# Scores of both key halves as one run of twelve products in a top-k attention and maxout kernel

## The chip, the cores and the metric

The kernel runs on one core of a Trainium2 chip. Its engines are TensorE (PE in the rows, with its weight loads as PEld), VectorE (DVE), ScalarE (ACT), GpSimd (POOL) and SyncE (SP, which issues the transfers). The metric is the device time of one execution in microseconds.

## The reference

Attention keeps the 32 largest scores of each row and drops the others; a three-way maxout layer and an output layer follow.

```python
def _attn_ref(q, k, v):                      # 8 batches, 8 heads, 576 rows, head size 64
    B, H, S, D = q.shape
    top_k = 32
    scale = 1.0 / np.sqrt(D)
    scores = scale * np.matmul(q, k.transpose(0, 1, 3, 2))
    kth = np.partition(scores, -top_k, axis=-1)[..., -top_k:-top_k + 1]
    mask = scores >= kth
    scores = np.where(mask, scores, -1000000000.0)
    scores = scores - np.max(scores, axis=-1, keepdims=True)
    attn = np.exp(scores)
    attn = attn / (np.sum(attn, axis=-1, keepdims=True) + 1e-09)
    return np.matmul(attn, v).astype(np.float32)

def _moe_ref(x, w1, w2, w3, w_out):          # x 4608 x 512, w1 to w3 512 x 768, w_out 768 x 512
    h = np.maximum(np.maximum(x @ w1, x @ w2), x @ w3)
    return (h @ w_out).astype(np.float32)
```

## The kernel before

The attention is cut into 160 units, 20 in each batch: four pairs of heads times five query tiles. The first four tiles of a pair hold 128 queries of each of its two heads (a full unit); the fifth holds the last 64 queries of both heads in one tile of 128 rows (a narrow unit). Unit 70, of which rows of the order are shown below, is the first tile of the third head pair of the fourth batch.

A unit goes through these steps, with the letter that the planner's table gives each and the line that does the work:

- **q, scores (L511).** The 576 keys are taken in two halves of 288. One half is six matmuls: for each of two heads the products high·high, high·low and low·high of split queries and keys. A half fills one score tile in PSUM, 128 x 2 x 512 floats, of which 288 columns of each head are used. There are two such tiles (the ring `s`), so that two halves are in flight at most.
- **e, copies (L522; L525 to L529 for a narrow unit)** by ACT, from the score tile to SBUF, one for each half. **s, sweeps (L539)** by DVE: the eight largest of every 72 keys, eight MAX8 for each half of a full unit, read from the score tile itself. A narrow unit's sweeps read the copies. A score tile is free again when its copy and, in a full unit, its sweep are done.
- **N, p1 to p5 (L545 to L570):** a pivot for each row out of the sweeps, on POOL and DVE. **g (L577, ACT), w (L582, POOL), k (L586, DVE):** signs of the scores against the pivot, the scores below it, their eight largest. **i, j, h (L594 to L606):** the 32nd largest is picked.
- **m, mask (L629, DVE)** and **x, exponential (L638, ACT)**; **d, r, z** (L645, L650, L657): the denominator.
- **T, transposes (L696, L691, L693, PE)**, **E, their copies (L711 to L716, ACT)**, **v, values (L741, PE)** for two full tiles together, **y, Y, Z** (L751 DVE, L756 ACT, L764 POOL): the row of x that the next layer reads, in two halves of fp16.

Before each pair of heads PE transposes its queries and keys (L454, L463). The maxout layer (L797) and the output layer (L857) of a batch are PE work with short steps on the other engines (L804 to L812, L862); they start when the x of their batch is there. The weights are decoded, measured and cut in two within the first units (L241 to L305).

The program's order is written out by a planner, `in_order`, when the kernel is built. Each step is a `Piece` with its engine, a cost in ns, the pieces that it needs, the rings that it takes a buffer of, and a rank (the unit's number plus an entry of `OFFSETS`). The planner keeps a clock for each engine, takes the piece that can start first, and lets a piece of lower rank go ahead of one that could start up to `PATIENCE` ns earlier. A piece that takes a buffer can start when that buffer's last readers are done by the planner's clock. The two layers' pieces are a list of their own, `fill`, from which PE takes when no piece of the attention can start soon enough. PE's pieces have a mode: `rows` for the scores (64 rows of the array for each of two heads), `columns` for the values, none for the rest; a change of mode costs `SWITCH` ns in the plan. DVE pieces marked `alone` (p4 on L568, the masks on L629) are planned to start no earlier than POOL's end plus `LOCK_A`, which is negative. Each engine then runs its own list in that order, and waits by semaphores.

In `attention`, which writes the pieces of one unit, each half of the scores is a piece of 393 ns that takes one buffer:

```python
        for i in range(2):
            rel = []
            takes = [("s", rel)]
...
            p(("q", i), "PE", 393, lambda i=i: qk(n, i), needs=needs, takes=takes, mode="rows")
```

Of the kernel before, what the change touches and what calls it, by code (L numbers as in the profile page):

```python
# [30 lines left out]
SWITCH = 95.0  # L31
WINDOW = 150
LEAD = 8.0
LOCK_A = -150.0
LOCK_B = -100.0
OFFSETS = {'x1': 0.96, 'j': 0.85, 'i': 0.48, 'N': 0.29, 'w1': -0.04, 'e1': -1.05, 'y': 0.91, 's1': 0.01, 'v': -0.12, 'u': -0.09, 'p1': -0.14, 'g0': 0.06, 'h': -0.01, 'E2': 0.48}
RANK_P = -3.5
RANK_R = 4.0
AHEAD = 4
RANK_W = (-2.0, 0.0, 1.0, 4.0)  # L40
RANK_V = -12.0
# [85 lines left out]
        left -= 1  # L127


PATIENCE = {'PE': 119.0, 'DVE': 50.0, 'ACT': 0, 'POOL': 50.0, 'SP': 0.0}  # L130


@with_exitstack
def kernel(ctx, tc, q, k, v, moe_w1, moe_w2, moe_w3, moe_w_out, out):
# [350 lines left out]
    books = {}  # L485
# [13 lines left out]
    def qk(n, i):  # L499


        b, hp, u = units[n]
        qT, kT = T_of[b, hp]
        if i == 0:
            open_unit(n)
        s = ps_s.tile([P, 2, 512], F32, name="s")
        for n_, (qa, ka) in enumerate(((0, 0), (0, 1), (1, 0))):
            for h in range(2):
                sl = slice(64 * h, 64 * h + 64)
                c0 = u * P if u < NU else S - 64 * (1 + h)  # L510
                nc.tensor.matmul(s[:, h, :HALF], qT[sl, qa, c0:c0 + P], kT[sl, ka, i * HALF:(i + 1) * HALF], start=(n_ == 0),  # L511
                                 stop=(n_ == 2))
        st[n]["s"].append(s)
# [385 lines left out]
    n = len(units)  # L899
# [5 lines left out]
    preps, starts, prep_of = [], [], []  # L905
# [5 lines left out]
    def attention(n):  # L911

        b, hp, u = units[n]
        nt = 2 if u < NU else 1
        full = nt == 2
        g = group_of.get(n, [n])
        opens, closes = n == g[0], n == g[-1]
        d = of[n] = {}
        p = lambda key, *a, **kw: d.setdefault(key, piece(*a, rank=n + OFFSETS.get(key if isinstance(key, str) else key[0] + str(key[1]), 0.0), **kw))
        for i in range(2):  # L920
            rel = []
            takes = [("s", rel)]
            needs = list(prepared[prep_of[n]])
            if i == 0 and b not in opened:
                opened[b] = []
                takes.append(("books", opened[b]))
            if i:
                needs.append(d["q", 0])
            p(("q", i), "PE", 393, lambda i=i: qk(n, i), needs=needs, takes=takes, mode="rows")
            p(("e", i), "ACT", 519 if full else 700, lambda i=i: evac(n, i), needs=[d["q", i]] + ([d["e", 0]] if i else []),  # L930
              takes=[] if i else [("ssb", held(n, "ssb"))])
            p(("s", i), "DVE", 1112 if full else 536, lambda i=i: sweep(n, i),
              needs=([d["q", i]] if full else [d["e", 1] if x else d["e", 0] for x in range(2)] if i else [])
              + ([d["s", 0]] if i else []), takes=[] if i else [("L", held(n, "L"))])
            rel.append(d["e", i])
            if full:
                rel.append(d["s", i])
# [21 lines left out]
        for t in range(nt):  # L959
            p(("m", t), "DVE", 820, lambda t=t: mask(n, t), needs=[d["h"]], alone=True)  # L960
            p(("x", t), "ACT", 760, lambda t=t: expo(n, t), needs=[d["m", t], d["p2"]] + ([d["x", 0]] if t else []),
              takes=[] if t else [("pm", held(n, "pm")), ("rs", held(n, "rs")), ("sums", held(n, "sums"))])
# [11 lines left out]
        for i in range(3):  # L974
            if i == 1 and not full:
                continue
            rel = []
            p(("T", i), "PE", 436 if i < 2 else 218, lambda i=i: turn(n, i),
              needs=[xs[i]] + last_v if i < 2 else [*xs, d["z"], *([] if full else [d["u"]]), *last_v], takes=[("tr", rel)])
            first = opens and i == 0  # L980
            p(("E", i), "ACT", 466 if i < 2 else 264 if full else 453, lambda i=i: turned(n, i),
              needs=[d["T", i]] + ([] if i == 0 else [d["E", 0]]), takes=[("pT", held(g[0], "pT"))] if first else [])
# [6 lines left out]
        rel, takes = [], []  # L989
        needs = [x for k in g for key, x in of[k].items() if key[0] == "E"] + [scaled_v[b], loaded_v[b, hp]]  # L990
# [18 lines left out]
    def held(n, *key):  # L1009
        return holders.setdefault((n, *key), [])  # L1010
# [104 lines left out]
    with tc.If(redo != 0):  # L1115
        with tc.For_i(0, B, 1) as b:
# [6 lines left out]
            for hp in range(NP):  # L1123
# [5 lines left out]
                for u in range(NU + 1):  # L1129
                    i = len(units)  # L1130
# [52 lines left out]
```

## Time and profile before

| | us |
|---|---|
| median of 2 runs | 1374.88 (1374.14 to 1375.62) |
| the profiled execution | 1373.02 |
| its span, first to last instruction | 1371.2 |
| PE busy | 1212.2 (88%) |
| DVE busy | 1200.0 (88%) |
| ACT busy | 1115.9 (81%) |
| POOL busy | 989.1 (72%) |

The span is what the views below divide. 1.8 us of the execution's time lie outside it. The busy time of an engine is a sum over its instructions, and stretches of the program differ: the first 150 us hold the weights, the last 70 us only the two layers of the last batch.

### The profile page before, as it was taken

The numbers are of one execution on the slowest core, as the hardware profiler recorded it, in microseconds if no ns is written. First come the engines' busy times: TensorE is split into PE (matmuls) and PEld (weight loads), VectorE is DVE, ScalarE is ACT, GpSimd is POOL, SyncE is SP. The second block draws the span as 40 slices with busy tenths as digits, with TensorE's granted clock in tenths as the row PEclk, the third lists the DMA queues.
The fourth block names the chain that finished last, engine by engine and source line by source line (L and its number), as shares of the span: only waits on it lengthen the run. The fifth ranks groups of instructions, "written<-read, shape, count | busy, mean of one in ns | idle before, by whom it ended". The sixth has DMA issues, their size and how long they took to land.

```text
span 1371.2 us, 32398 instructions
## 1 busy us (share of the span) xinstructions
PE 1212.2 (88%) x9981; PEld 859.8 (63%) x9981; DVE 1200.0 (88%) x5928; ACT 1115.9 (81%) x2732; POOL 989.1 (72%) x1669
## 2 busy tenths in 40 slices
PE   2331699899689999999999999999999999999997
PEld 1221477566467675676777676767676767776775
DVE  6797798999989999999999999999999999999621
ACT  3556799888898898898988899989988999898721
POOL 2779887678777787786787777778778768686511
PEclk9965899999789999999999999999999999999999
DMA  6341010211101011111111110201020101100000
GB/s 214 114 144 34 3 36 19 60 28 27 43 2 44 27 43 34 27 27 44 27 43 28 43 24 22 60 24 46 9 53 25 36 19 41 27 9 1 17 17 27
DMA packets 107893, 53.69 MB, mean 39 GB/s; under 512 B 91840, under 2 KB 100032, under 8 KB 107712
## 3 DMA queue, kind: packets, MB, share of 16 engines
q1 hardware_dynamic: 107712, 51.54, 13.9%
q8 instruction: 81, 1.33, 0.4%
q14 instruction: 100, 0.82, 0.2%
HBM read 42.07 MB, written 9.44 MB: 38 GB/s over the span
## 4 chain that ended last, share of the span: by engine, by line
PE 60%; DVE 19%; ACT 13%; POOL 3%; issue 3%; SPq 1%; DMA 0%; ACTq 0%; DVEq 0%; POOLq 0%
PE m L797 24%; PE tr L741 9%; PE s L511 9%; PE m L857 8%; PE tr L696 7%; DVE L L539 6%; DVE ssb L629 3%; ACT pm L638 3%; ACT w L577 3%; DVE Q L586 2%; ACT pT L711 2%; ACT ssb L522 2%; PE tr L463 2%; DVE ob L242 1%; PE tr L691 1%
## 5 line engine op out<-in xcount | busy, mean ns | idle before, releaser
L582 POOL TENSOR_TENSOR w<-ssb,w 128x576 f32<-128x576 f32 x288 | 416.3, 1450 | 57.3 <-ACT w L577 53.2
L797 PE MATMUL m<-xh,wall 128*128 128x256 f16 (+2 forms) x2448 | 438.3, 279 | 0.7 <-ACT ob L862 0.4
L797 PEld LDWEIGHTS <-wall 128*128 128x128 f16 x3672 | 339.4, 98 | 84.2 <-issue 14.5
L797 PE MATMUL m<-xl,wall 128*128 128x256 f16 (+2 forms) x1224 | 335.3, 279 | 0.3 <-POOL xl L764 0.3
L539 DVE MAX8 L<-s 128x8 f32<-128x72 f32 x2048 | 307.3, 223 | 19.9 <-ACT ssb L522 9.9
L629 DVE SCALAR_TENSOR_TENSOR ssb<-ssb,kth 128x576 f32<-128x576 f32 x288 | 257.1, 908 | 1.0
L638 ACT ACTIVATE pm<-ssb,nb 128x576 f32<-128x576 f32 x288 | 223.9, 778 | 27.0 <-DVE ssb L629 24.1
L511 PE MATMUL s<-kT,qT 64*128 64x288 f32 x1920 | 210.8, 334 | 32.6 <-ACT ssb L522 16.5
L586 DVE MAX8 Q<-w 128x8 f32<-128x576 f32 x288 | 214.9, 749 | 18.1 <-POOL w L582 18.0
L577 ACT ACTIVATE w<-ssb,Q 128x576 f32<-128x576 f32 x288 | 222.7, 777 | 9.5 <-DVE Q L570 4.9
L711 ACT COPY pT<-tr 128x512 f32<-128x512 f32 (+1 forms) x416 | 210.1, 521 | 20.8 <-PE tr L696 15.1
L696 PE MATMUL tr<-ident,pm 128*128 128x128 f32 x1152 | 182.0, 287 | 26.4 <-ACT pm L638 19.2
L511 PEld LDWEIGHTS s<-kT,qT 64*128 64x128 f32 x1920 | 144.3, 194 | 96.9 <-ACT ssb L522 28.5
L522 ACT COPY ssb<-s 128x576 f32<-128x576 f32 x256 | 161.5, 642 | 33.3 <-DVE L L539 17.0
L741 PE MATMUL tr<-pT,vt 128*64 128x256 f32 (+1 forms) x1920 | 183.2, 338 | 3.3 <-ACT pT L716 2.0
L696 PEld LDWEIGHTS tr<-ident,pm 128*128 128x128 f32 x1152 | 133.4, 145 | 73.3 <-ACT pm L638 32.6
L806 DVE SCALAR_TENSOR_TENSOR h<-m,rises,h 128x256 f32<-128x256 f32 (+2 forms) x204 | 100.6, 493 | 66.5 <-PE m L797 61.9
L741 PEld LDWEIGHTS tr<-pT,vt 128*64 128x64 f32 x1920 | 110.2, 139 | 66.0 <-issue 18.9
L812 POOL TENSOR_TENSOR hl<-h,hh 128x256 f16<-128x256 f32 (+2 forms) x102 | 78.1, 766 | 75.3 <-ACT hh L809 73.0
L857 PE MATMUL m<-wall,hh 128*128 128x512 f16 x432 | 128.9, 380 | 0.0
L657 POOL TENSOR_SCALAR rsw<-rs 128x128 f32<-128x128 f32 x160 | 63.8, 400 | 38.5 <-DVE rs L650 10.9
L645 POOL TENSOR_SCALAR den<-sums 128x2 f32<-128x2 f32 (+1 forms) x160 | 41.1, 257 | 60.6 <-ACT pm L638 51.4
(124 smaller groups left out, 1863.7 us busy)
## 6 DMA issues: line engine op xcount, KB each, us to landing
qt<-in_q_dram SPq DMA_DIRECT2D x68, 128.0 KB, 2.9
kt<-in_k_dram SPq DMA_DIRECT2D x68, 128.0 KB, 3.0
out_dram<-ob SPq DMA_DIRECT2D x32, 256.0 KB, 2.3
wall<-in_moe_w_dram SPq DMA_DIRECT2D x6, 768.0 KB, 6.0
vt<-in_v_dram SPq DMA_DIRECT2D x32, 128.0 KB, 2.4
xh<-in_moe_w_dram SPq DMA_DIRECT2D x6, 384.0 KB, 4.8
xl<-in_moe_w_dram SPq DMA_DIRECT2D x6, 384.0 KB, 5.6
vt<-in_v_dram SPq DMA_DIRECT2D x32, 64.0 KB, 2.2
```

The lines of the kernel that those rows point to most:

```text
L511: nc.tensor.matmul(s[:, h, :HALF], qT[sl, qa, c0:c0 + P], kT[sl, ka, i * HALF:(i + 1) * HALF], start=(n_ == 0), stop=(n_ == 2))
L539: nc.vector.max(d["L"][:, t, g, :], d["s"][i][:, t, g0:g0 + GW] if d["nt"] == 2 else d["ssb"][0][:, g * GW:(g + 1) * GW])
L577: nc.scalar.activation(d["w"][t], d["ssb"][t], AF.Sign, bias=d["Q"][:, t, 0:1], scale=-1.0, accum_out=d["cnt"][:, t:t + 1])
L582: nc.gpsimd.tensor_tensor(d["w"][t], d["ssb"][t], d["w"][t], ALU.mult)
L586: nc.vector.max(d["Q"][:, t, 1:NW], d["w"][t])
L629: nc.vector.scalar_tensor_tensor(ss, ss, d["kth"][:, t:t + 1], ss, ALU.is_lt, ALU.subtract, accum_out=d["lost"][:, t:t + 1])
L638: nc.scalar.activation(d["pm"][:, t], d["ssb"][t], AF.Exp, bias=d["nb"][:, t:t + 1], scale=-1.0 / SHRINK, accum_out=d["sums"][:, t:t + 1])
L696: nc.tensor.transpose(pt[:, j * P:(j + 1) * P], pm[:, i, 64 * i + j * P:64 * i + (j + 1) * P], ident)
L711: nc.scalar.copy(pT[:, 512 * i:512 * i + m] if i < 2 else pT[:, 8 * P:10 * P], pt[:, :m])
L741: nc.tensor.matmul(xp[64 * h:64 * h + 64, :m], vt[:, 4 * h + i if i < 4 else 8 + h, :], keys(i, h), start=(i == 0), stop=(i == 4))
L797: nc.tensor.matmul(box["ps", i][:, :c1 - c0], a, bb[:, kc, c0:c1], start=(kc == 0 and k == 0), stop=(kc == KC - 1 and k == 2))
L857: nc.tensor.matmul(box["po"][:n], a[:, f, cs], bb, start=(f == 0 and k == 0), stop=(f == FC - 1 and k == 2))
```

## The change

The two pieces of six matmuls become one piece of twelve, `q0`, of 786 ns, which takes both score tiles at once: the planner places it where the last readers of both are done. Copies and sweeps of both halves need this one piece; a tile is still handed back for each half by itself. With it come other numbers of the planner: nine entries of `OFFSETS` are new or changed, `RANK_R` (the rank of a batch's review) goes from 4.0 to 2.4, PE's `PATIENCE` from 119 to 155, and `LOCK_A` from -150 to -248. No instruction is added or removed on any engine; their order changes on all of them. Counted in the part of the program that is executed (the part behind the flag `redo` is not), PE's mode goes to rows 258 times before and 160 times in the changed kernel: 44 and 32 times up to unit 32, 214 and 128 times after it. It goes to columns 96 times in both. Behind the last values stand 102 maxout matmuls of the last batch's first part (256 columns) before and 78 in the changed kernel; everything else behind them is the same.

```diff
--- before.py
+++ after.py
@@ -31,11 +31,11 @@
 SWITCH = 95.0
 WINDOW = 150
 LEAD = 8.0
-LOCK_A = -150.0
+LOCK_A = -248.0
 LOCK_B = -100.0
-OFFSETS = {'x1': 0.96, 'j': 0.85, 'i': 0.48, 'N': 0.29, 'w1': -0.04, 'e1': -1.05, 'y': 0.91, 's1': 0.01, 'v': -0.12, 'u': -0.09, 'p1': -0.14, 'g0': 0.06, 'h': -0.01, 'E2': 0.48}
+OFFSETS = {'q0': -1.0, 'x1': -0.22, 'j': 0.85, 'i': 0.48, 'N': 0.29, 'w1': -0.04, 'e1': -1.05, 'y': 0.91, 's1': 0.01, 'v': 0.45, 'u': -0.7, 'p1': -0.14, 'g0': 0.06, 'h': -0.01, 'E2': 0.44, 'e0': 0.81, 'T2': 0.12, 'p2': -0.36, 'w0': 0.24}
 RANK_P = -3.5
-RANK_R = 4.0
+RANK_R = 2.4
 AHEAD = 4
 RANK_W = (-2.0, 0.0, 1.0, 4.0)
 RANK_V = -12.0
@@ -127,7 +127,7 @@
         left -= 1
 
 
-PATIENCE = {'PE': 119.0, 'DVE': 50.0, 'ACT': 0, 'POOL': 50.0, 'SP': 0.0}
+PATIENCE = {'PE': 155.0, 'DVE': 50.0, 'ACT': 0, 'POOL': 50.0, 'SP': 0.0}
 
 
 @with_exitstack
@@ -917,21 +917,18 @@
         opens, closes = n == g[0], n == g[-1]
         d = of[n] = {}
         p = lambda key, *a, **kw: d.setdefault(key, piece(*a, rank=n + OFFSETS.get(key if isinstance(key, str) else key[0] + str(key[1]), 0.0), **kw))
-        for i in range(2):
-            rel = []
-            takes = [("s", rel)]
-            needs = list(prepared[prep_of[n]])
-            if i == 0 and b not in opened:
-                opened[b] = []
-                takes.append(("books", opened[b]))
-            if i:
-                needs.append(d["q", 0])
-            p(("q", i), "PE", 393, lambda i=i: qk(n, i), needs=needs, takes=takes, mode="rows")
+        rels, takes = [[], []], []
+        if b not in opened:
+            opened[b] = []
+            takes.append(("books", opened[b]))
+
+        d["q", 0] = d["q", 1] = p("q0", "PE", 786, lambda: [qk(n, i) for i in range(2)], needs=list(prepared[prep_of[n]]),
+                                  takes=takes + [("s", rel) for rel in rels], mode="rows")
+        for i, rel in enumerate(rels):
             p(("e", i), "ACT", 519 if full else 700, lambda i=i: evac(n, i), needs=[d["q", i]] + ([d["e", 0]] if i else []),
               takes=[] if i else [("ssb", held(n, "ssb"))])
             p(("s", i), "DVE", 1112 if full else 536, lambda i=i: sweep(n, i),
-              needs=([d["q", i]] if full else [d["e", 1] if x else d["e", 0] for x in range(2)] if i else [])
-              + ([d["s", 0]] if i else []), takes=[] if i else [("L", held(n, "L"))])
+              needs=([d["q", i]] if full else []) + ([d["s", 0]] if i else []), takes=[] if i else [("L", held(n, "L"))])
             rel.append(d["e", i])
             if full:
                 rel.append(d["s", i])
```

PE's list before, around the two halves of unit 70 (`s<-kT,qT` are the scores, `tr<-pT,vt` values, `tr<-ident,kt` a transpose of keys, `m<-` the maxout layer):

```order
L797 LDWEIGHTS wall
L797 MATMUL m<-xl,wall 128x256
L511 MATMUL s<-kT,qT_108 128x288 x6
L741 MATMUL tr<-pT,vt_89 64x64 x10
L511 MATMUL s<-kT,qT_108 128x288 x6
L463 MATMUL tr<-ident,kt 128x128 x4
L797 LDWEIGHTS wall
```

PE's list in the changed kernel, at the same unit (`tr<-ident,pm` and `tr<-ident,rsw` are transposes of a unit before, `hl` belongs to the output layer):

```order
L857 LDWEIGHTS hl
L857 MATMUL m<-wall,hl 128x512
L696 MATMUL tr<-ident,pm 128x128 x4
L691 MATMUL tr<-ident,pm 128x128
L693 MATMUL tr<-ident,rsw 128x128
L511 MATMUL s<-kT,qT_108 128x288 x12
L454 MATMUL tr<-ident,last 128x128
```

The twelve products stand in one row, and the values that came between them have gone elsewhere.

DVE's list before, from the first sweep of unit 70 on (`L<-s`, eight MAX8; the sweep of its second half comes 17 rows after it):

```order
L539 MAX L<-s 128x8 x8
L650 RECIPROCAL rs<-den 128x2
L629 SCALAR_TENSOR_TENSOR ssb,lost<-ssb,kth 128x576 x2
L806 SCALAR_TENSOR_TENSOR h_9731<-m,rises,h_9690 128x256
L557 MAX n_9742<-nA 128x8 x2
L559 TENSOR_REDUCE nb<-nA 128x2
L553 MAX b_0_114<-L 128x8
L563 MATCH_REPLACE nR<-n_9742,nA 128x32 x2
L565 MAX n_9742<-nR 128x8 x2
L806 SCALAR_TENSOR_TENSOR h_9760<-m,rises,h_9731 128x256
L842 TENSOR_SCALAR so_9766<-back_wi,back_wo,back_v 128x1
L843 TENSOR_SCALAR so_9765<-so_9766 128x1
```

DVE's list in the changed kernel, around both sweeps of unit 70:

```order
L629 SCALAR_TENSOR_TENSOR ssb,lost<-ssb,kth 128x576 x2
L539 MAX L<-ssb 128x8 x4
L539 MAX L<-s 128x8 x8
L586 MAX Q<-w 128x8
L553 MAX b_0_114<-L 128x8
L539 MAX L<-s 128x8 x8
L806 SCALAR_TENSOR_TENSOR h_9859<-m,rises,h_9815 128x320
L650 RECIPROCAL rs<-den 128x2
```

Two rows stand between the sweeps of the two halves where there were sixteen. Over the last 98 full units of each program the mean is 4.3 rows in the changed kernel and 6.7 before; between ACT's copies of the two halves it is 1.6 and 3.8.

## Rows read from the trace of the kernel before

**Rows 1.** Windows: stretch, length, busy us (instructions) of PE, PEld, DVE, ACT, POOL; PEclk.

```profile
0.00:150.00 150.00, 51.04 (x252) 32.23 (x252) 114.55 (x396) 81.47 (x173) 106.39 (x165) 0.78 0.38 116
...
324.00:560.00 236.00, 212.74 (x1686) 146.24 (x1684) 217.93 (x1144) 210.07 (x517) 180.65 (x301) 0.94 0.14 36
560.00:797.00 237.00, 234.25 (x1999) 169.07 (x1995) 226.05 (x1161) 213.76 (x530) 179.53 (x309) 1.00 0.12 31
797.00:1034.00 237.00, 232.89 (x1960) 166.82 (x1958) 224.71 (x1162) 214.78 (x534) 184.37 (x311) 1.00 0.14 34
1034.00:1270.00 236.00, 233.71 (x1934) 165.14 (x1933) 221.76 (x1141) 206.66 (x509) 177.38 (x305) 1.00 0.09 23
...
350.00:400.00 50.00, 35.65 (x249) 24.91 (x249) 42.51 (x224) 44.11 (x107) 36.48 (x61) 0.77 0.09 20
```

**Rows 2.** Chain that ended last, in time: start us, us, what.

```profile
1159.18 0.59 PE s L511 x6
1159.77 1.42 PE m L797 x12
...
1161.30 0.99 PE s L511 x12
1162.29 0.26 PE tr L691
...
1168.82 0.11 PE tr L691
1169.04 1.31 PE m L797 x12
...
1177.08 0.58 PE tr L696 x4
...
1178.32 0.44 PE tr L463 x4
```

**Rows 3.** Waits of DVE, 324 to 1270 us: us in total, times, longest.

```profile
DVE h L806 <- PE m L797: 12.7, 33, 1.6
DVE xs L751 <- PE tr L741: 9.0, 15, 1.5
DVE L L539 <- PE s L511: 5.6, 9, 2.1
```

**Rows 4.** The same chain at its end.

```profile
1300.16 0.73 PE tr L741 x20
...
1320.01 23.58 PE m L797 x216
```

**Rows 5.** Timeline of PE: start us, us, instruction, [idle before <- releaser].

```profile
347.23 0.67 PE L511 MATMUL s<-kT,qT 64*128 64x288 f32 x6
351.21 1.09 PE L511 MATMUL s<-kT,qT 64*128 64x288 f32 x6 [3.31 <-ACT ssb L522]
...
399.48 0.67 PE L511 MATMUL s<-kT,qT 64*128 64x288 f32 x6
```

**Rows 6.** Windows of the scores' line alone: PE, PEld.

```profile
560.00:797.00 237.00, 40.02 (x384) 26.90 (x380) 1.00 0.12 31
```

**Rows 7.** Timelines of PE, DVE and ACT around the scores of units 121 and 122.

```profile
987.03 0.67 PE L511 MATMUL s<-kT,qT 64*128 64x288 f32 x6
...
990.52 0.66 PE L511 MATMUL s<-kT,qT 64*128 64x288 f32 x6
...
988.05 1.20 DVE L539 MAX8 L<-s 128x8 f32<-128x72 f32 x8
...
991.15 0.64 ACT L522 COPY ssb<-s 128x576 f32<-128x576 f32 x1 [1.23 <-DVE L L539]
```

**Rows 8.** Waits of PE for a score tile, 324 to 1270 us.

```profile
PE s L511 <- ACT ssb L522: 11.3, 12, 3.3
```

**Rows 9.** DVE's pieces marked alone: count, ns min/median/max.

```profile
L629 DVE SCALAR_TENSOR_TENSOR ssb<-ssb,kth x288: 789/814/2021, 37.5 to 1291.3; 128x576 f32<-128x576 f32 x144
...
L568 DVE SCALAR_TENSOR_TENSOR z<-n,b x160: 139/167/1416, 24.6 to 1285.4; 128x16 f32<-128x16 f32 x128, 128x8 f32<-128x8 f32 x32
```

## The prediction

> **What bounds the kernel now.** I read the windows first, to see the stages apart [rows 1]. Up to 150 us the weights are decoded; PE works 51.0 us of 150 and what it saves there is worth nothing. From 324 to 560 us it is idle for 23.3 us of 236. From 560 to 1270 us it is idle for 2.8, 4.1 and 2.3 us, 9.2 us in 710. From 1270 on it does not stop until the attention ends at 1300.16 + 0.73, near 1301 us [rows 4]. DVE is next: from 324 to 1270 us it is busy 217.9 + 226.1 + 224.7 + 221.8 = 890.5 us of 946, 94.1%, with 55.5 us idle. ACT stands near 90% and POOL near 76%. So two engines are almost full, PE a little more than DVE, and a saving on PE can be spent until DVE is full.
>
> Then the chain of waits, in order of time, to see what PE pays for the scores. Six matmuls that follow a transpose or the maxout layer take 0.59 us on it, twelve in one run 0.99 us [rows 2]. The second six therefore cost 0.40 us and the first six 0.59: entering costs 0.19 us. Leaving costs too: twelve maxout matmuls behind scores take 1.42 us against 1.31 elsewhere, one transpose 0.26 against 0.11, four transposes 0.58 against 0.44 [rows 2]. That is 0.10 to 0.15 us. One visit to the scores' mode costs 0.29 to 0.34 us beyond its work; I take 0.31.
>
> **The change part by part.** *Fewer visits.* The order has 258 entries into the mode before and 160 in the changed kernel, 98 fewer; 12 of them lie in the first 32 units, which end near 324 us, and 86 behind them. In the first part PE waits for others in any case, and I count nothing. Behind it, 86 x 0.31 = 26.7 us of PE's time go away (24.9 and 29.2 us with the two ends). No operation is added.
>
> *What comes to be late instead.* PE needs 946 - 26.7 = 919 us for the stretch if its idle time stays. DVE's work there is 890.5 us, and it keeps the idle time that is not PE's doing. DVE waited for PE 12.7 + 9.0 + 5.6 = 27.3 us [rows 3]; the other 55.5 - 27.3 = 28.2 us were waits for ACT and POOL and the joints between instructions. With all of its waits for PE gone, DVE would need 890.5 + 28.2 = 919 us as well. So both engines could just give 27 us, but only if both were full at 97 to 98% in the same order, and no wait for ACT or POOL grew. The other end is nothing at all, for which one stretch speaks. From 345 to 400 us PE has no maxout work, and it is idle 14.4 of the 50 us behind 350 [rows 1]. If a crowded PE held the attention back, units should come faster there. Fifteen score pieces start from 347.23 to 399.48 us [rows 5], 52.25 / 14 = 3.73 us each, 7.46 us for a unit. In the full stretch from 560 us, 384 score matmuls are 32 units in 237 us [rows 6], 7.41 us each. PE's idle time bought nothing there, though it was one stretch and the granted clock was 0.77 on average in it, between its levels of 1.2 and 2.4 GHz. Between 0 and -27 us I take the middle, **-14 us**, since the waits on PE are real but a good part will be waited for on the next engine.
>
> *The tail.* Behind the last values PE does only the last batch's layers, back to back. 102 matmuls of 256 columns of its first part are left there, and 78 in the changed kernel. 216 of them take 23.58 us [rows 4], 0.109 us each, so 24 fewer end the kernel **2.6 us** earlier. The rest behind it is the same.
>
> *Two tiles at once.* This is the part that costs. A score tile is refilled soon after it is free: the sweep of the first half of unit 121 ends at 988.05 + 1.20 = 989.25 us, and the next unit's first half starts on that tile at 990.52; the second half's tile is free only with ACT's copy at 991.15 + 0.64 = 991.79 us [rows 7]. In the changed kernel nothing of unit 122 could start before 991.79, 1.27 us later. What hides this is DVE's backlog of other work: a unit needs 2 x 1.2 us of sweeps, and a period of 7.41 us leaves it 5 us for masks, pivots and maxima of earlier units. The order answers to it, with both sweeps and both copies standing closer (the mean of 6.7 rows between sweeps becomes 4.3). PE fills the time with the maxout layer as before. I price it at nothing in the forecast; the price without that cover is in the third rival.
>
> *The numbers of the planner.* `PATIENCE`, `RANK_R` and the offsets add and remove no work. They move pieces, and their effect is in the counts above as far as PE goes. Up to unit 32 they might also move the weights' steps; the window up to 150 us has 35 us of idle DVE time [rows 1], and I know no reason for either sign, so I put plus or minus 5 us there into the range. `LOCK_A` is priced with the fourth rival.
>
> Sum: -14 - 2.6 = -16.6 us, 1373.0 - 16.6 = 1356.4 us for an execution like the profiled one. The median lies 1.9 us over that execution, so I forecast **1358 us**. The range of this case alone is 1350 to 1366 us.
>
> **The rivals.** *PE is the bound throughout.* All 26.7 us come back, and the tail's 2.6: 1374.9 - 29.3 = 1346 us, 1343 to 1347.5 with the ends of the price. For it speaks that PE is idle 9 us in 710; against it, DVE would have to run at 97%, which it does in no window of [rows 1], the highest being 95.4%.
>
> *Others set the pace.* The visits that PE saves become idle time, and only the tail's 2.6 us remain: 1372 us, or 1367 to 1378 with the 5 us of the first part. The stretch without maxout work speaks for it [rows 5, 6]. The Trainium skill says in "Perfetto Trace Analysis", under Identifying the Most-Contended Engine, that matmul busy time is a poor measure of how near TensorE is to its limit and that weight-load busy time should be read instead. By that rule PE would not be the bound here: its weight loads are busy 70% from 560 to 1270 us [rows 1], DVE then leads at 94 to 95%, and the sum would be this rival's 1372 us. The chain of waits does not agree with the rule where maxout matmuls stand: 216 in 23.58 us leave no gap [rows 4].
>
> *The two tiles starve PE or DVE; slower.* If both tiles are not free when PE comes to the run, PE stands still, and DVE behind it has no scores to sweep. Such waits exist now: 12 of PE's waits for the copy that frees a tile sum to 11.3 us, 0.94 us each, the longest 3.3 [rows 8]; [rows 5] show that one. If half of the 128 runs behind unit 32 met such a wait, 64 x 0.94 = 60 us would be lost against 29.3 saved: 1374.9 + 31 = 1406 us. It decides from 29.3 / 128 = 0.23 us for each run, a wait at every fourth; over 0.45 us the kernel is slower by more than 2%. For it speaks how soon a tile is refilled today. Against it, the planner places the run where both tiles are free by its clock, the new order brings the sweeps together, and only 12 such waits of PE in 946 us show today.
>
> *DVE is shut out longer.* `LOCK_A` goes from -150 to -248, so that the planner may place DVE's pieces marked alone 98 ns earlier before POOL's end. Today they are blocked now and then: the masks' median is 814 ns and their longest 2021, the pivot's 167 and 1416 [rows 9]. If each of the 448 pieces (288 masks, 160 pivots) stood blocked for 98 ns more, DVE would lose 44 us, 35 us of it behind unit 32, where four fifths of the pieces lie. Taken with the forecast's -16.6 that gives 1374.9 + 18.5 = 1393 us. Against it, the medians lie close to the minima of 789 and 139 ns, so most pieces meet no such block. The Trainium skill names the mechanism in "SBUF — State Buffer", under Who interferes with whom: a DVE instruction with two inputs in SBUF and a GpSimd one that reads SBUF take an exclusive lock, and whichever comes second waits for the whole of the first. By that rule planning closer to POOL's end gains nothing and can only add blocked time on DVE, up to this rival's sum; the trace agrees as far as the longest of [rows 9] go.
>
> That the products don't come to stand together is no rival, since the order shows 160 runs of twelve.
>
> **How the numbers follow.** The chances: forecast 0.36, PE the bound 0.20, others set the pace 0.27, starved by two tiles 0.10, shut out 0.07. The likeliest gives 1358 us. A range from 1340 to 1384 us holds the first three, with most of the 5 us of the first part, and leaves out the last two, 0.17. Two per cent, about what a measurement of this kernel can tell from no change, is 1347.4 us and 1402.4 us: faster by more is the first rival, 0.20; slower by more is the third, 0.10; the forecast, the second and the fourth lie between, 0.70.
>
> **What would show it.** In the profile of the changed kernel, every run of scores should read x12 with about 0.99 us on the chain, and the busy time of PE should fall by some 25 to 30 us from 1212. If PE is the bound throughout, its idle time from 324 us to the end of the attention stays near 32 us, and DVE's falls to 28 us or less. If others set the pace, PE's idle time there grows to nearly 60 us and the attention still ends near 1300 us; by the forecast it ends near 1287 us. If the two tiles starve PE, its waits for ACT's copy and DVE's sweep at the scores rise from 11 us to 40 and more. If DVE is shut out, the masks' median rises from 814 ns. I should be wrong altogether if the weights' stage moves by more than 10 us, or if the maxout work runs out for PE in more places than the one near 350 us, since the clock granted to PE fell there.

## The result, and the profile after

The changed kernel took 1390.31 us (median of 2 runs, 1388.46 to 1392.16) against 1374.88 (median of 2). The quotient of these two medians is 1.0112. The ratio on record with the result, which all that follows uses, is 1.0135, with an interval from 1.0103 to 1.0167; it puts the kernel before near 1372 us, where five later sets of runs had it too (1369 to 1372). By either figure the kernel is slower, where 1358 us and a range of 1340 to 1384 were forecast.

First the windows of the changed kernel, in the stretches and columns of [rows 1]; the row behind the dots is a new place.

```profile
0.00:150.00 150.00, 48.08 (x232) 30.57 (x232) 122.42 (x400) 81.05 (x172) 108.12 (x164) 0.77 0.38 116
324.00:560.00 236.00, 214.92 (x1723) 151.16 (x1723) 216.53 (x1116) 206.60 (x508) 174.52 (x296) 0.93 0.13 33
560.00:797.00 237.00, 225.00 (x1908) 164.72 (x1907) 220.09 (x1107) 205.14 (x503) 179.84 (x297) 0.98 0.13 33
797.00:1034.00 237.00, 225.78 (x1879) 161.99 (x1877) 220.82 (x1140) 211.10 (x524) 179.74 (x306) 0.96 0.12 32
1034.00:1270.00 236.00, 229.22 (x1943) 165.84 (x1942) 219.72 (x1136) 204.95 (x505) 177.72 (x299) 1.00 0.10 26
...
650.00:700.00 50.00, 42.36 (x330) 28.64 (x329) 43.87 (x224) 45.36 (x115) 35.35 (x59) 0.93 0.11 30
```

From 560 to 1270 us PE stands idle for 12.0, 11.2 and 6.8 us, 30 us where it was 9.2. But DVE has not filled up in exchange: it is busy 660.6 us of these 710 instead of 672.5. Both engines do less in the same time. The windows of the scores' line alone say how much less, against [rows 6]:

```profile
560.00:797.00 237.00, 33.03 (x362) 25.73 (x364) 0.98 0.13 33
```

362 score matmuls in 237 us instead of 384: 30.2 units where there were 32.

The change did what it says. On the chain of the changed kernel, in order of time, the scores read as in [rows 2], but only in runs of twelve, and the end reads as in [rows 4]:

```profile
1160.93 0.99 PE s L511 x12
...
1171.79 0.98 PE s L511 x12
1176.77 0.59 PE tr L696 x4
1177.35 1.01 PE s L511 x12
...
1322.05 0.73 PE tr L741 x20
1322.78 2.07 PE m L797 x18
1324.96 6.55 PE m L797 x60
...
1339.28 23.58 PE m L797 x216
```

The last values end at 1322.8 us instead of 1300.9. The 18 + 60 = 78 matmuls behind them are there. The waits of DVE and then of PE, 324 to 1270 us, answer to [rows 3] and [rows 8]:

```profile
DVE Q L586 <- POOL w L582: 16.7, 22, 3.0
DVE xs L751 <- PE tr L741: 13.7, 16, 2.3
DVE L L539 <- ACT ssb L522: 13.2, 18, 1.7
DVE h L806 <- PE m L797: 6.2, 13, 1.3
DVE L L539 <- PE s L511: 1.8, 3, 1.2
```

```profile
PE tr L691 <- ACT pT L711: 10.5, 12, 3.2
PE tr L696 <- ACT pm L638: 9.1, 13, 2.5
PE tr L691 <- ACT raws L457: 8.6, 4, 2.6
...
PE s L511 <- ACT ssb L522: 1.2, 3, 0.7
```

DVE's waits for PE fell from 27.3 to 21.7 us (13.7 + 6.2 + 1.8), so PE did get out of its way a little. PE's wait for a score tile almost vanished, 11.3 to 1.2 us: the order no longer asks for a tile too early. It asks later. PE's idle time now stands before transposes instead; that these belong to units that started late is my reading of it. DVE's waits for POOL and for ACT's copies grew, against these rows of the kernel before:

```profile
DVE L L539 <- ACT ssb L522: 4.6, 9, 1.2
DVE Q L586 <- POOL w L582: 4.3, 8, 0.9
```

The busy times, with the groups of the sweeps, masks, scores and copies of the changed kernel (busy us, mean ns, idle time just before them and what ended it), from its page:

```profile
PE 1208.3 (87%) x9981; PEld 869.6 (63%) x9981; DVE 1216.9 (88%) x5928; ACT 1117.3 (80%) x2732; POOL 995.8 (72%) x1669
...
L539 DVE MAX8 L<-s 128x8 f32<-128x72 f32 x2048 | 306.5, 220 | 25.4 <-ACT ssb L522 16.5
L629 DVE SCALAR_TENSOR_TENSOR ssb<-ssb,kth 128x576 f32<-128x576 f32 x288 | 267.7, 945 | 1.4
...
L522 ACT COPY ssb<-s 128x576 f32<-128x576 f32 x256 | 160.6, 642 | 47.7 <-DVE L L539 31.7
L511 PE MATMUL s<-kT,qT 64*128 64x288 f32 x1920 | 187.2, 327 | 12.4 <-POOL qT L472 3.4
```

and the same two readers of a score tile, sweeps and copies, on the page of the kernel before:

```profile
L539 DVE MAX8 L<-s 128x8 f32<-128x72 f32 x2048 | 307.3, 223 | 19.9 <-ACT ssb L522 9.9
...
L522 ACT COPY ssb<-s 128x576 f32<-128x576 f32 x256 | 161.5, 642 | 33.3 <-DVE L L539 17.0
```

The scores' own matmuls became 23.6 us cheaper (210.8 to 187.2). The copies waited for sweeps 31.7 us instead of 17.0, and the sweeps for copies 16.5 instead of 9.9.

One refill of the changed kernel, from its timelines of PE, DVE and ACT (in that order: start us, us, instruction). It is an extreme one: ACT's order brings the copies ten microseconds behind the sweeps, so the tiles are held for 15 and 16 us, where the mean is 5.6.

```profile
923.38 1.06 PE L511 MATMUL s<-kT,qT 64*128 64x288 f32 x12
940.05 1.06 PE L511 MATMUL s<-kT,qT 64*128 64x288 f32 x12
...
924.90 1.20 DVE L539 MAX8 L<-s 128x8 f32<-128x72 f32 x8
926.68 1.20 DVE L539 MAX8 L<-s 128x8 f32<-128x72 f32 x8
...
937.81 0.62 ACT L522 COPY ssb<-s 128x576 f32<-128x576 f32 x1
939.45 0.64 ACT L522 COPY ssb<-s 128x576 f32<-128x576 f32 x1
```

The first tile is free at 937.81 + 0.62 = 938.43 us. Nothing can be put into it before the second copy ends at 940.09, and the next run starts there. With two pieces the first half could have started 1.6 us earlier.

### The profile page after: what moved, and what is told of

The parts are those of the page before. It is cut to its first block, busy times and chain, and to the rows that moved or that the text cites. A ratio compares the mean times of both kernels' runs of the same rounds, so it can differ in the third digit from the quotient of the medians.

```text
span 1390.4 us, 32408 instructions
## 1 busy us (share of the span) xinstructions
PE 1208.3 (87%) x9981; PEld 869.6 (63%) x9981; DVE 1216.9 (88%) x5928; ACT 1117.3 (80%) x2732; POOL 995.8 (72%) x1669
## 3 DMA queue, kind: packets, MB, share of 16 engines
q1 hardware_dynamic: 107712, 51.54, 13.7%
## 4 chain that ended last, share of the span: by engine, by line
PE 51%; DVE 26%; ACT 14%; POOL 4%; issue 3%; DMA 0%; SPq 0%; ACTq 0%; DVEq 0%; POOLq 0%
PE m L797 21%; PE tr L741 8%; DVE L L539 7%; PE m L857 6%; PE s L511 6%; PE tr L696 6%; DVE ssb L629 4%; ACT pm L638 3%; DVE Q L586 3%; ACT pT L711 3%; ACT w L577 2%; ACT ssb L522 2%; DVE ob L242 2%; DVE wall L243 2%; PE tr L463 1%
## 5 line engine op out<-in xcount | busy, mean ns | idle before, releaser
L797 PEld LDWEIGHTS <-wall 128*128 128x128 f16 x3672 | 343.8, 98 | 80.7 <-issue 8.0
L539 DVE MAX8 L<-s 128x8 f32<-128x72 f32 x2048 | 306.5, 220 | 25.4 <-ACT ssb L522 16.5
L629 DVE SCALAR_TENSOR_TENSOR ssb<-ssb,kth 128x576 f32<-128x576 f32 x288 | 267.7, 945 | 1.4
L586 DVE MAX8 Q<-w 128x8 f32<-128x576 f32 x288 | 215.1, 749 | 22.5 <-POOL w L582 21.8
L696 PE MATMUL tr<-ident,pm 128*128 128x128 f32 x1152 | 186.1, 290 | 36.2 <-ACT pm L638 19.0
L522 ACT COPY ssb<-s 128x576 f32<-128x576 f32 x256 | 160.6, 642 | 47.7 <-DVE L L539 31.7
L511 PE MATMUL s<-kT,qT 64*128 64x288 f32 x1920 | 187.2, 327 | 12.4 <-POOL qT L472 3.4
L741 PE MATMUL tr<-pT,vt 128*64 128x256 f32 (+1 forms) x1920 | 191.7, 348 | 4.2 <-ACT pT L711 3.7
L696 PEld LDWEIGHTS tr<-ident,pm 128*128 128x128 f32 x1152 | 132.9, 146 | 86.8 <-ACT pm L638 33.0
L741 PEld LDWEIGHTS tr<-pT,vt 128*64 128x64 f32 x1920 | 115.2, 144 | 72.5 <-issue 20.7
L764 POOL TENSOR_TENSOR xl<-xs,xh 128x256 f16<-128x256 f32 (+1 forms) x96 | 66.3, 690 | 36.4 <-ACT xh L756 32.7
```

The costliest lines, as they stand in the source:

```text
L539: nc.vector.max(d["L"][:, t, g, :], d["s"][i][:, t, g0:g0 + GW] if d["nt"] == 2 else d["ssb"][0][:, g * GW:(g + 1) * GW])
L586: nc.vector.max(d["Q"][:, t, 1:NW], d["w"][t])
L629: nc.vector.scalar_tensor_tensor(ss, ss, d["kth"][:, t:t + 1], ss, ALU.is_lt, ALU.subtract, accum_out=d["lost"][:, t:t + 1])
L696: nc.tensor.transpose(pt[:, j * P:(j + 1) * P], pm[:, i, 64 * i + j * P:64 * i + (j + 1) * P], ident)
L741: nc.tensor.matmul(xp[64 * h:64 * h + 64, :m], vt[:, 4 * h + i if i < 4 else 8 + h, :], keys(i, h), start=(i == 0), stop=(i == 4))
L797: nc.tensor.matmul(box["ps", i][:, :c1 - c0], a, bb[:, kc, c0:c1], start=(kc == 0 and k == 0), stop=(kc == KC - 1 and k == 2))
```

## The experiments

**How the runs are measured.** Every time is a median, set against runs of the kernel before on the same chip (1369 to 1372 us in the five sets). Five figures more are worked out from each trace. The *unit period* is the time from the first score matmul of unit 32 to that of unit 159, over 127. The *empty time* of a score tile runs from the end of its last reader to the next score matmul into it, the mean of the 254 refills behind unit 32, and the *held time* is the rest of its cycle. These two make up the period by definition (within 0.06 us, as the held time is averaged over two tiles more), so they say where it went, not why. *Idle* is that stretch less busy time. *Visits* are the scores' entries in PE's rows.

| run | us | ratio and interval | period us | empty / held us | idle PE / DVE us | visits |
|---|---|---|---|---|---|---|
| (before, one profile) | 1374.88 | 1 | 7.445 | 1.10 / 6.36 | 32 / 56 | 258 |
| (changed, one profile) | 1390.31 | 1.0135, 1.0103 to 1.0167 | 7.645 | 2.05 / 5.57 | 54 / 73 | 160 |
| merged_old | 1403.38 | 1.0243, 1.0226 to 1.0261 | 7.787 | 2.07 / 5.69 | 56 / 81 | 160 |
| split_new | 1375.74 | 1.0042, 1.0025 to 1.0059 | 7.421 | 1.04 / 6.37 | 25 / 58 | 268 |
| coupled_old | 1394.51 | 1.0187, 1.0167 to 1.0207 | 7.577 | 2.37 / 5.21 | 49 / 69 | 198 |
| jitter | 1396.79 | 1.0197, 1.0180 to 1.0214 | 7.558 | 0.97 / 6.57 | 47 / 71 | 255 |
| jit_old93 | 1390.67 | 1.0135, 1.0080 to 1.0191 | 7.522 | 1.18 / 6.31 | 38 / 67 | 253 |
| jit_old96 | 1387.37 | 1.0111, 1.0057 to 1.0166 | 7.601 | 1.05 / 6.53 | 34 / 65 | 260 |
| jit_new97 | 1389.74 | 1.0129, 1.0067 to 1.0190 | 7.617 | 2.08 / 5.57 | 51 / 75 | 160 |
| jit_new93 | 1392.22 | 1.0147, 1.0091 to 1.0203 | 7.629 | 2.09 / 5.53 | 51 / 73 | 160 |
| jit_sn97 | 1379.02 | 1.0063, 1.0043 to 1.0083 | 7.400 | 0.96 / 6.50 | 29 / 58 | 266 |
| jit_sn93 | 1375.65 | 1.0035, 1.0020 to 1.0050 | 7.392 | 1.06 / 6.36 | 28 / 47 | 261 |
| parted_new | 1422.56 | 1.0380, 1.0363 to 1.0397 | 7.823 | 2.62 / 5.18 | 45 / 97 | 311 |
| gathered_old | 1401.58 | 1.0235, 1.0205 to 1.0265 | 7.700 | 1.71 / 5.97 | 58 / 88 | 214 |
| coupled_new | 1406.53 | 1.0251, 1.0221 to 1.0280 | 7.713 | 2.45 / 5.24 | 52 / 76 | 194 |
| moved_up | 1376.34 | 1.0027, 1.0010 to 1.0045 | 7.486 | 0.96 / 6.53 | 40 / 59 | 234 |
| copy_split | 1378.18 | 1.0044, 1.0030 to 1.0058 | 7.393 | 0.99 / 6.44 | 33 / 58 | 241 |
| copy_new | 1361.84 | 0.9926, 0.9903 to 0.9949 | 7.426 | 1.99 / 5.41 | 35 / 58 | 158 |
| copy_split97 | 1365.00 | 0.9954, 0.9934 to 0.9973 | 7.529 | 1.00 / 6.51 | 23 / 58 | 246 |
| copy_new97 | 1354.52 | 0.9885, 0.9859 to 0.9911 | 7.364 | 2.00 / 5.34 | 31 / 55 | 158 |

**The two parts of the change apart.** merged_old is the run of twelve with the planner's numbers of before; split_new is the two pieces with the new numbers, the offset of the run given to both.

```diff
 merged_old, against the changed kernel
-LOCK_A = -248.0
+LOCK_A = -150.0
...
 (OFFSETS, RANK_R and PATIENCE as before)
```

```diff
 split_new, against the kernel before
-LOCK_A = -150.0
+LOCK_A = -248.0
-OFFSETS = {'x1': 0.96, ...
+OFFSETS = {'q0': -1.0, 'q1': -1.0, 'x1': -0.22, ...
...
 (RANK_R and PATIENCE as in the change)
```

> One run of twelve that takes both score tiles, with all the planner's numbers of the kernel before. Tiles theory (a run that takes both tiles holds back the next unit until the slower tile is free; the unit period goes from 7.41 to 7.6 us or more): 1385 us or more. Numbers theory (the offsets, LOCK_A and the rest cost the time, the run itself saves visits): 1346 to 1372 us. Chance theory (any new order costs or gains some 10 us): anywhere from 1360 to 1390 us.

> Two pieces of six with one tile each, as before, with the changed kernel's numbers (the offset -1.0 of the run is given to both pieces). Tiles theory: 1378 us or less, since each tile is refilled when it is free. Numbers theory: 1388 us or more. Chance theory: anywhere from 1360 to 1390 us.

Measured 1.0243 and 1.0042. Against the order of the kernel before, the new numbers alone cost 0.4%, the run alone 2.4%, and with the run the new numbers take back nearly half of that. That order is a lucky one, as the reshuffled orders below show, so the 2.4% is too high a price for the run. `LOCK_A` is in split_new too, and the masks stay at 257.6 us on its page (257.1 before, 267.7 in the changed kernel), so `LOCK_A` alone does not make the masks longer.

**The coupling without the run.** Two pieces, but the first takes both tiles, so that other work may still come between the halves.

```diff
-        for i in range(2):
-            rel = []
-            takes = [("s", rel)]
+        rels = [[], []]
+        for i, rel in enumerate(rels):
+            takes = [("s", r) for r in rels] if i == 0 else []
```

> Numbers of the kernel before, and two pieces of six that other work may come between, but the first takes both tiles and the second none: the coupling of the tiles without the saved visits. Tiles theory: the coupling's price bare, 1395 us or more, above the run of twelve with the same numbers by some 10 us or more for the visits that are not saved. Numbers theory: 1375 us, within 5. Chance theory: 1360 to 1390 us.

The same edit with the new numbers is coupled_new.

> Split pieces with the changed kernel's numbers, but the first takes both tiles and the second none; other work may come between. If the coupling of the tiles costs the time: 1388 us or more, unit period 7.6 us, a free tile idle for 2 us. If it is the uninterrupted run: 1374 to 1381 us, as split_new and its two neighbours.

Measured 1.0187 and 1.0251, with the tiles empty for 2.37 and 2.45 us. With the new numbers taking the tiles together is enough for the loss: two pieces without the coupling lie at 1.0035 to 1.0063. That the twelve products are uninterrupted is not its cause. coupled_old proves less, since it lies within the scatter of the old numbers' reshuffled orders (1.0111 to 1.0197). It was also expected 10 us or more above merged_old and came out 9 us below, while coupled_new is 16 us above the run with the same numbers (1.0135). For coupled_new 9 of the 16 us stand ahead of unit 32 (335.5 us instead of 326.6 in the mean of three), and its 34 visits more would be 7 by the price that parted_new gives below; the difference of sign stays open.

**How much is the order's chance.** `SWITCH`, another of the planner's costs, moved a little shifts every later decision and changes no work.

```diff
-SWITCH = 95.0
+SWITCH = 97.0
```

That is jitter, on the kernel before. The others do the same with 93, 96 or 97 on the kernel before (jit_old), on the changed kernel (jit_new) and on split_new (jit_sn).

> The kernel before with SWITCH 97 in place of 95, which changes the order without a reason of its own: how far time moves with the order alone. Chance theory: 8 us or more away from 1375. Tiles and numbers theories: within 6 us of 1375.

> The kernel before with SWITCH 93: a second reshuffled order of the split pieces, after SWITCH 97 gave 1396.8 us against 1369.7. Chance theory (the kernel before has a lucky order, and orders of either kind scatter around one mean): 1385 to 1405 us. Tiles theory (split orders are faster than coupled ones in the mean by 10 us or more, since a free tile waits 1.0 us for its refill and not 2.0): 1370 to 1390 us, idle time of a free tile near 1.0 us.

> The kernel before with SWITCH 96, a third such order. Chance theory: 1385 to 1405 us. Tiles theory: 1370 to 1390 us, idle time of a free tile near 1.0 us.

> The changed kernel with SWITCH 97: a reshuffled order of the runs of twelve. Chance theory: 1385 to 1405 us, the same mean as the reshuffled split orders. Tiles theory: 1395 to 1415 us, above them, with a free tile idle for 2 us before its refill.

> The changed kernel with SWITCH 93, a second such order. Chance theory: 1385 to 1405 us. Tiles theory: 1395 to 1415 us, a free tile idle for 2 us.

> The split pieces with the changed kernel's numbers (1375.7 us) and SWITCH 97: was that order lucky too. If the changed kernel's numbers suit split pieces: 1370 to 1382 us. Chance theory (reshuffled split orders lie at 1387 to 1397): 1385 to 1400 us.

> The same with SWITCH 93. If the changed kernel's numbers suit split pieces: 1370 to 1382 us. Chance theory: 1385 to 1400 us.

With the old numbers the order matters more than the change does: three neighbours of the kernel before are 1.1 to 2.0% slower than it, so it is an uncommonly good draw, and the changed kernel is no slower than they are on average (1.0148). So far the chance theory holds, with 1385 to 1405 us for all of these, and the tiles theory, with 1395 to 1415 for the runs, does not; the neighbours of split_new, at 1379 and 1376 us, speak against the chance theory. merged_old, at 1.0243, lies 0.9% above the same average. With the new numbers the orders differ little, which makes a fair comparison: three with two pieces have ratios of 1.0042, 1.0063 and 1.0035 (mean 1.0047), three with the run 1.0135, 1.0129 and 1.0147 (mean 1.0137). **The run costs 0.9%, 12 us,** in the mean of the three settings, 0.7 to 1.1% at each. Between the two families the period goes from 7.40 to 7.63 us, PE's idle time from 27 to 52 us, DVE's from 54 to 74. Over the whole span PE does 13.4 us less work with the run and stands idle for 28.3 us more.

**What a visit costs.** parted_new keeps the run's place in the plan and both tiles, but the second half is written behind PE's next piece (or where one of its readers comes).

```diff
+    def parted(n):
+        qk(n, 0)
+
+        def second():
+            waiting.remove(second)
+            qk(n, 1)
+        waiting.append(second)
...
-        d["q", 0] = d["q", 1] = p("q0", "PE", 786, lambda: [qk(n, i) for i in range(2)], ...
+        d["q", 0] = d["q", 1] = p("q0", "PE", 786, lambda: parted(n), ...
```

> The changed kernel with its order on every other engine as it is; on PE alone the second six products come one piece later, behind the piece that followed the run. Nothing is reshuffled; PE goes to rows some 300 times and not 160. Visits theory (PE is the bound, 0.31 us each): 40 us or more slower than the changed kernel, 1425 us or more. If what PE saves or spends is lost in other waits: within 8 us of the changed kernel, 1382 to 1398 us. Between, the share tells how much of PE's time counts.

1.0380 against the run's 1.0135: 33.6 us for 151 visits, 0.22 us each. It delays the second half as well, so this leans to the high side. But PE's busy time rose with the visits, from 1208.3 to 1247.3 us: visits do count.

**The run without waiting in the plan.** gathered_old keeps the plan of before, and writes the second half right behind the first where its tile is free by then; else the first is held back to the second. moved_up does the moving up alone.

```diff
+    def gathered(n, i):
+        if i == 0 or len(st[n]["s"]) == 1:
+            qk(n, i)
+        users = rings["s"].users
+        if i == 0 and len(users) > 1 and all(y.start is not None for y in users[-2]):
+            qk(n, 1)
...
-            p(("q", i), "PE", 393, lambda i=i: qk(n, i), needs=needs, takes=takes, mode="rows")
+            p(("q", i), "PE", 393, lambda i=i: gathered(n, i), needs=needs, takes=takes, mode="rows")
```

(moved_up; gathered_old has, for `i == 0` with its second tile still held, nothing written until the second half or a reader comes.)

> The kernel before with its order on every other engine as it is; on PE the two halves of a unit are brought together, the second moved up where its tile is free by then, else the first held back to the second, unless a copy or sweep of the first comes between. Some 45 visits fewer. Visits theory: 14 us faster, 1356 us. If saved visits are not worth anything: 1368 to 1373 us. Tiles theory (what a tile loses by standing empty costs more than the visits): 1380 us or more.

> The kernel before with its order on the other engines as it is; on PE the second half of a unit is moved up behind the first where all readers of its tile stand ahead in the program, some 25 visits fewer, nothing held back. Visits theory at 0.2 us each (what parted_new lost for each added one): 5 us faster, 1365 us. If PE then stands and waits for the tile: 1372 us or more.

moved_up has 24 visits fewer and no gain, 1.0027: PE is idle for 7 us more, and its waits for the copy that frees a tile went from 11.3 to 14.6 us. gathered_old has 44 fewer and costs 32 us. On its page the sweeps and the copies wait for the scores themselves:

```profile
L557 DVE MAX8 L<-s 128x8 f32<-128x72 f32 x2048 | 307.0, 221 | 39.4 <-PE s L511 27.7
...
L539 ACT COPY ssb<-s 128x576 f32<-128x576 f32 x256 | 161.8, 641 | 52.9 <-PE s L511 24.9
```

A first half held back is missed by both its readers at once.

**A tile with one reader.** copy_new is the changed kernel with the sweeps reading ACT's copy in SBUF, so that the copy alone frees a tile; copy_split is the same on split_new. copy_new97 and copy_split97 have `SWITCH` at 97.

```diff
-                nc.vector.max(d["L"][:, t, g, :], d["s"][i][:, t, g0:g0 + GW] if d["nt"] == 2 else d["ssb"][0][:, g * GW:(g + 1) * GW])
+                nc.vector.max(d["L"][:, t, g, :], d["ssb"][t][:, g * GW:(g + 1) * GW])
...
-              needs=([d["q", i]] if full else []) + ...
+              needs=([d["e", i]] if full else []) + ...
...
-            if full:
-                rel.append(d["s", i])
```

> The changed kernel with the same edit. Tiles theory: with tiles held for a shorter time the coupling stops to bind, the run's 100 saved visits remain, and it comes within 5 us of copy_split or below it. If the uninterrupted run is the cause: it stays 10 us or more above copy_split.

> split_new with the sweeps of full units reading the copy in SBUF, as a narrow unit's do, so that a score tile is free after ACT's copy alone. All results are computed. Tiles theory: little changes, 1365 to 1385 us, since a split order has tiles enough; a tile is held for 4 us or less and not 6.4.

> copy_new with SWITCH 97. If its gain is the edit's: 1358 to 1367 us, 10 us or more below copy_split97. If it was one lucky order: 1370 us or more.

> copy_split with SWITCH 97. By the tiles theory 1374 to 1382 us, above copy_new97 by the visits that the run saves, 10 us or more. If the order of copy_split was an unlucky one: 1370 us or less.

Now the run is the faster one: 1361.84 against 1378.18 us, and 1354.52 against 1365.00. The mean ratios are 0.9906 with the run and 0.9999 with two pieces, so the run brings 0.94%, 13 us, where it cost 12. Only two settings stand behind it, 0.9% apart for the pieces and 0.4% for the run; the sign is the same in both. copy_new97 beats the kernel before by 1.15% and the changed one by about 2.5%, as the ratio of their two ratios. The unit period shows the gain in one pair only: it goes from 7.393 to 7.426 us in the first and from 7.529 to 7.364 in the second, since an order also decides how much maxout work is left behind the last values (the tails take 72.9 and 65.1 us in the first pair, 64.5 and 63.8 in the second). PE's whole span shows it in both. PE has 18 us less work with the run in either pair, and stands idle for 1.7 and 8.2 us more, where the run with two readers idled 28.3 us more. On the page of copy_new the two readers do not wait for one another any more:

```profile
L539 DVE MAX8 L<-ssb 128x8 f32<-128x72 f32 x2304 | 336.4, 218 | 8.7 <-ACT ssb L522 8.5
...
L522 ACT COPY ssb<-s 128x576 f32<-128x576 f32 x256 | 159.1, 642 | 5.5 <-PE s L511 4.4
```

The copies wait 5.5 us instead of 47.7; the sweep takes 218 ns a piece from SBUF, as from PSUM (all 2304 in one form here, the narrow units' among them). In its windows, with the columns of [rows 1] and then of [rows 6], the stretch in which the changed kernel lost most against before has most of PE's work back, and 384 score matmuls as before:

```profile
560.00:797.00 237.00, 231.16 (x1982) 171.12 (x1980) 221.68 (x1173) 212.47 (x529) 183.86 (x308) 0.98 0.12 31
...
560.00:797.00 237.00, 34.75 (x384) 27.13 (x384) 0.98 0.12 31
```

The tiles are still empty for 1.99 us between units, as in every coupled order: emptiness alone is not the cost. It goes with a longer period when the time that a tile is held does not shrink as much. From pieces to run the empty time grows by 1.0 us with either kind of sweep; the held time falls by 0.85 us where sweep and copy both read the tile (6.41 to 5.56, means of three) and by 1.1 us where the copy alone does (6.48 to 5.38, means of two). Held for less than 4 us, as I had thought a tile with one reader might be, it is in none of the four: the copies too come when their engine's order has them.

## Why the prediction was wrong, step by step

**Fewer visits.** The count was right, 258 to 160, and so, roughly, was the price: 0.31 us forecast; 23.6 us less on the scores' group over 98 visits is 0.24, and parted_new paid 0.22. Not all of it stayed: values and transposes (L741, L696) took 8.5 and 4.1 us more on the changed page, with a mean granted clock of 0.944 instead of 0.961, so PE's busy time fell by 3.9 us, not 25 to 30. (The lower clock is not what makes the kernel slow: its other execution had 0.971 and took 1388.46 us. jit_new93 took 1393.09 us at 0.939 and 1391.35 at 0.968.) Against the family of split_new, the fairer comparison, it fell by 13.4 (1225.1 to 1211.7, means of three).

**What comes to be late instead** (-14 us): this term came out with the other sign. Its full end asked that no wait for ACT or POOL grew; DVE's waits for POOL at L586 went from 4.3 to 16.7 us, and those for ACT's copies at L539 from 4.6 to 13.2. From unit 32 to unit 159 the changed kernel took 970.9 us instead of 945.5, 25.4 more. What PE saved became idle time, as in the second rival, and more than that was lost.

**The tail** (-2.6 us): 70.3 to 67.6 us behind the last values, right in size. But its 24 matmuls fewer were no separate gain, and the tail moves with any order (59.3 us in jit_new97, 75.4 in split_new). Between the families the 127 periods take 28.7 us more; from the last unit's scores to the last values 7.4 us come back, behind the values 9.8, and the first 32 units take 3.7 more: 28.7 + 3.7 - 7.4 - 9.8 = 15 us between the profiled spans. The likely reason, which no run tests, is that slower units leave PE time for maxout work earlier, so that less is left for the end.

**Two tiles at once**: the step that failed. "I price it at nothing in the forecast", because DVE's backlog and the maxout layer would hide it. Its 1.27 us at unit 121 was about the right cost for one refill, and the mean empty time grew by 1.0 us. It was not hidden. The backlog covers a sweep that comes late, but the pace also hangs on the ring: a tile's cycle of empty and held time is the unit's period, and the held time gave back only 0.85 of 1.05. The rest, 0.2 us by these means and 0.23 by the period, is the 28.7 us of the 127 periods above, of which the ends take 17 back. Where the term held nothing, PE stands idle for 28 us more than with two pieces and the same numbers.

**The numbers of the planner**: unit 32 starts 1.9 us later, within the 5. Over the whole kernel split_new and its two neighbours put them at +0.3 to +0.6%, which I had not forecast; with the run's 0.9% they make the 1.35%. That the order of before is 1.1 to 2.0% better than its own neighbours, so that a new order was likely to lose something whatever the change, was not in the sum either.

**The rivals.** *PE is the bound throughout* is refuted by 52 us of idle time on PE. *Others set the pace* had the sign of the idle time right (near 60 forecast, 54 found), but let the attention end near 1300 us; it ended at 1322.8. The rule of the Trainium skill in "Perfetto Trace Analysis", Identifying the Most-Contended Engine, is that weight-load busy time should be read and not matmul busy time; by it PE would not have been the bound. The changed kernel does not decide on it, since there the coupling lost more than the visits saved. Two runs speak against it: more visits cost 0.22 us each in parted_new, at the same number of weight loads, and fewer visits gave 0.94% once the tile had one reader.

*The two tiles starve PE or DVE; slower* was the right mechanism with the wrong sign to look for. I expected PE's waits for a tile to go from 11 to 40 us; they went to 1.2. The argument against it, "the planner places the run where both tiles are free by its clock", is how the time is lost: the wait is in the order, and shows as a longer period. Its point of decision, 0.23 us for each run, is where loss and savings cancel. The period grew by 0.20 us over that of before with the savings already in it, so the loss was well past that point.

Why two readers matter is shown by the four copy runs. On the changed kernel's page copies and sweeps wait for each other for 31.7 + 16.5 = 48.2 us, on split_new's for 17.3 + 15.3 = 32.6, on copy_new's for 8.5, all of it for data. With the neighbours the first two are 40.1 and 29.8 us, means of three. In the traces of before, changed and split_new the copy and the sweep of a half never overlap, in none of 256 halves; the smallest gap between them is 31 ns. The Trainium skill, in "PSUM — Partial Sum Buffer", PSUM bank collisions raise a hardware error, says that two engines may not touch the same partitions of one bank at the same time, readers included, and that the compiler's scheduler adds a dependency between them. The trace agrees with this: a copy waits for a sweep, and a sweep for a copy, though neither writes the tile.

*DVE is shut out longer* is not it, by split_new. Its sign did not come: the masks' median stays at 814 ns, as the row of the changed kernel shows, with the columns of [rows 9].

```profile
L629 DVE SCALAR_TENSOR_TENSOR ssb<-ssb,kth x288: 790/814/3696, 37.0 to 1315.5; 128x576 f32<-128x576 f32 x144
```

A few masks do take longer, the longest 3696 ns where it was 2021. In the runs they come to 262.7 us against 255.3 (means of three), which may be part of the loss; why is open.

**What is open.** Why the kernel before is 16 to 27 us better than its own neighbours. That the old numbers suffer more from the run (merged_old, 1.0243) may be no more than this: against those neighbours it is 0.9% slower, as the new numbers' runs are against theirs, but it is one order. One reader was tried at two settings of `SWITCH` only. `LOCK_A` alone on the numbers of before, and a third score tile, were not tried.

## What to carry to other kernels

A piece that takes every buffer of a ring at once makes each buffer wait for the last reader of all, and in a planned order the engine that fills the buffers may show no wait for them at all: look at the period and at how long a buffer stands empty. Before joining pieces, cut the readers of the buffer to one; here the same join cost 12 us with two and gave 13 with one. Compare families of orders, not two orders: here a cost moved by 1 or 2% changed the time by up to 2%.

## What the runs showed of the hardware

A MAX8 of 72 floats took 218 ns from SBUF (copy_new) and 220 to 226 from PSUM (changed kernel, before, split_new), so moving the sweeps cost DVE nothing. ACT and DVE read one score tile one after the other, never at once (0 of 256 halves). The granted clock fell where PE ran short of work: 0.93 from 650 to 700 us on average, between its levels of 1.2 and 2.4 GHz, in the changed kernel with PE busy for 42.4 of 50 us, in a stretch that before had 1.00 with PE busy for 49.6:

```profile
650.00:700.00 50.00, 49.64 (x394) 33.70 (x393) 48.15 (x240) 45.97 (x112) 40.27 (x66) 1.00 0.10 25
```
